# Retention attention and two mixtures of experts on one core: stores of x issued by POOL, copies of the x sums placed behind a block's layer 1 output, fewer staged pieces in expert 0, gate units at other places

## The chip, the cores and the metric

One core of a Trainium2 chip. Its engines are PE (matrix products), DVE, ACT and POOL (elementwise work) and SP, whose queue only issues transfers. Each engine takes its instructions strictly in order. The metric is the device time of one execution in microseconds (us).

## The reference

float32 throughout. The heads of the retention layer are laid side by side as 2304 rows of 512 and go through a dense mixture of 4 experts and then a routed one of 8, in which each row takes the expert of its largest logit.

```python
# retention, 4 batches, 8 heads, 576 positions, 64 wide
ret = scale * q @ k.T * Dmat          # Dmat[i, j] = gamma_h ** (i - j) for i >= j, else 0
x = (ret @ v)  ->  rows (2304, 512)
# mixture 1: 4 experts, all rows through each (512 -> 1024 -> 512)
for e in range(4):
    out += p[:, e:e+1] * (np.maximum(x @ w1[e], 0) @ w2[e])
# mixture 2: 8 experts, each row through one
logits = x @ w_gate; e_idx = argmax(logits); gate_w = softmax(logits)[e_idx]
eom = sigmoid(x @ w_output_gate)
out[mask] = gate_w * eom[:, e] * (np.maximum(x[mask] @ w1[e], 0) @ w2[e])
```

## The kernel before

**Numbers.** A float32 value is kept as a high and a low float16 part (`hi`, `lo`): ACT copies the high part, and POOL or DVE subtracts it from the value to get the low one. A product is three float16 products on PE.

**Blocks and units.** The 2304 rows are cut into 9 blocks of 256. Mixture 1 runs expert by expert, block by block. A block's layers are lists of units, a unit being some 12 to 24 matmuls. Blocks 0 to 4 of expert 0 use plain layers (`l1_first`, L518, and the second layer, L668); all later ones use layers with fewer products of sums and differences of quarters (`l1_mixed`, L546, and `l2_mixed`, L631), for which weights and x need such sums too. `keep` (L504, L505) takes a unit of layer 1 from PSUM: ACT writes the high part of ht (after the ReLU), DVE the low one.

**Attention inside expert 0.** The retention is computed in 36 steps of 64 positions, four steps to a block of x. Behind each unit of expert 0's first five blocks, `at_hook` runs one step s. It issues the loads of step s+4 on SP (qkr, vkr; five buffers), then `x_mix` of a block whose last step was s-1 (four subtractions on POOL, L347, that make the sums of x in place, `xf`), the step itself, `x_store` of the block's high and low parts (two steps behind its last), `x_keep` (three behind: the sums' high part by ACT, `xm`, L355, the low part by POOL, L356), and the second `x_store` (four behind). In a step PE takes the state of the past (L273), the scores of the next step (L250), their product with v (L286), and the next state (L301, from `ks`, which POOL scales, L229). DVE takes the step's result from PSUM as `xf` (L335), and ACT and POOL split it (L337, L339). The bank `uo` of a step is free for L273 of the next one once DVE has read it. Blocks of x later needed again are stored to DRAM as `xcd` (L359) and loaded by `x_load` (L383, or L385 and L386).

**Order.** A tile scheduler fixes the order on each engine before the run. A block `with tc.issue_after(i)` adds an edge: what is issued inside stands behind instruction i on the same engine. `pace` holds the last instruction of a kind for this. Other work is placed by tables of unit numbers: `w_plan` (weights of the next expert, with sums by POOL, `mix`, L449), `s_plan` (the weights of mixture 2, staged in pieces: load `sr`, two ACT instructions L200 and L201, one of DVE L202, store), and `gate_at` (units of mixture 2's gate and routing: `g1_rows`, `g1_turn`, `g2`, `g3a`, `g3b`). In the expert layers, POOL's L565, DVE's L569 and L606 and DVE's L639 (`acc`, the sum over experts) take units from PSUM.

Of the kernel before, what the change touches and what calls it, by code (L numbers as in the profile page):

```python
# [13 lines left out]
ACTF = mybir.ActivationFunctionType  # L14
ALU = mybir.AluOpType
# [11 lines left out]
NB = N // BT  # L27
# [16 lines left out]
BM = 5  # L44
# [86 lines left out]
def kernel(  # L131
# [19 lines left out]
    pe, act, dve, pool, sp = nc.tensor, nc.scalar, nc.vector, nc.gpsimd, nc.sync  # L151
# [58 lines left out]
    open_ctx = ExitStack()  # L210
    at_ps = [open_ctx.enter_context(tc.tile_pool(name="ps_1", bufs=2, space=PSUM))]
    ka = at_1.tile([128, ca.shape[1]], F32, name="ka", bufs=1)
    raws, pm, st, uos = {}, {}, {}, {}
    xcs, xfs, xos = {}, {}, {}

    def at_load(s):
        b, c = divmod(s, NC)
        a = at_raw.tile([128, 2, 4, C], F32, name="qkr")
        t = at_raw.tile([128, 2, 4, D], F32, name="vkr")
        sp.dma_start(out=a, in_=qk[b, c])  # L220
        sp.dma_start(out=t, in_=vk[b, c])
        raws[s] = a, t

    def at_split(s):
# [124 lines left out]
    def x_keep(b):  # L349
        m = xfs.pop(b)  # L350
        if xos[b][1] is None:
            xos[b][1] = at_1.tile([128, 2, 4, 2, HB], F16, name="xm", bufs=1)
        for i in range(2):
            hi, lo = [xos[b][1][:, a, 2 * i:2 * i + 2] for a in range(2)]
            act.activation(out=hi, in_=m[:, i], func=ACTF.Copy)  # L355
            pool.tensor_tensor(out=lo, in0=m[:, i], in1=hi, op=ALU.subtract)  # L356

    def x_store(b, i):
        sp.dma_start(out=xcd[b * 128:(b + 1) * 128, :, 4 * i:4 * i + 4], in_=xos[b][i])  # L359

    def at_step(s):

# [16 lines left out]
    def x_load(b, q, base=False):  # L379
        t = x_p.tile([128, 2, 8, 2, HB], F16, tag="xc", name="xc")  # L380
        src = xcd[b * 128:(b + 1) * 128]
        if base:
            q.dma_start(out=t[:, :, 0:4], in_=src[:, :, 0:4])  # L383
        else:
            q.dma_start(out=t[:, :, 0:2], in_=src[:, :, 0:2])  # L385
            q.dma_start(out=t[:, :, 3:], in_=src[:, :, 3:])  # L386
        xcs[b] = t
# [109 lines left out]

    hts = {}
    ops = {}
    pace = {}  # L500

    def keep(src, dst):

# [224 lines left out]
    def g1_rows(t, pl):  # L728

        xr = pl.tile([128, 2, DM], F16, tag="xr", name="xr")  # L730
        split_z(acc[:, t, 0:DM], xr[:, 0], xr[:, 1], S_X1)
        x1h[t] = xr

    def g1_turn(t, pl):
        xs = pl.tile([128, 2, KD, 128], F16, tag="xs", name="xs", bufs=2)
        sp.dma_start(
            out=xs.rearrange("p a k t -> p (a k) t"), in_=x1h[t].rearrange("p a d -> p (a d)"), transpose=True
        )
        x1h[t] = xs
# [478 lines left out]
    def s_plan(e, b, u):  # L1218
        if e == 0 and b <= BM:
            return  # L1220
        if b >= 2:
            if u in ((1, 3, 5, 7, 9, 12), (0, 3, 5, 7, 9), (0, 3, 5, 7, 9), (3, 5, 7, 9))[e] or (0 < e < 3 and b in (4, 6, 8) and u == 12):
                s_hook()
        elif b == 1 and u in (4, 6, 9):
            s_hook()
# [20 lines left out]
    def gate_plan(b):  # L1246
        ts = [b * TB + i for i in range(TB)]
        if b < NB - 3:
            for i, t in enumerate(ts):
                gate_at.setdefault((b + 2, i), []).append(lambda t=t: g1_rows(t, gp[0]))  # L1250
                gate_at.setdefault((b + 2, i + 1), []).append(lambda t=t: g1_turn(t, gp[0]))
                gate_at.setdefault((b + 2, i + 9), []).append(lambda t=t: g2(t))
            gate_at[b + 3, 2] = [lambda: g3a(b, gp[0])]
            gate_at[b + 3, 5] = [lambda: g3b(b, gp[0])]
        else:
            gate.extend(lambda t=t: g1(t, gp[0]) for t in ts)
            gate.extend(lambda t=t: g2(t) for t in ts)
            gate.append(lambda: g3a(b, gp[0]))
            gate.append(lambda: g3b(b, gp[0]))
            if b == NB - 3:  # L1260
                gate.append(go_early)

    prev = None
    for e in range(E1):
        for b in range(NB + (e == E1 - 1)):
# [16 lines left out]
            for u, unit in enumerate(units):  # L1282
                unit()
                z_from(e == 0 and b < BM and (b == 0 or u >= 4))
                if e == 0:
                    if u == 1 and b >= 2 or (b, u) == (1, 5):
                        x_load((b + 1) % NB, sp, base=b + 1 < BM)
                elif (e, b) == (1, 0):
                    if u == 0:
                        x_load(1, sp)  # L1290
                elif u == 0 and not last and (e, b) != (E1 - 1, NB - 1):
                    with tc.issue_after(pace["pool"].ins):
                        x_load((b + 1) % NB, pool)
                if e == 0:
                    for _ in range(1 + (b == 0 and u % 2)):
                        at_hook()
                if not last:
                    w_plan(e, b, u)
                    s_plan(e, b, u)
                if e == E1 - 1:  # L1300
                    for g in gate_at.pop((b, u), ()):
                        g()
                    if gate:
                        gate.pop(0)()
# [121 lines left out]
```

## Time and profile before

| | |
|---|---|
| median of 3 runs | 1043.08 us (1040.55 to 1043.15) |
| the profiled execution: its own time | 1045.07 us |
| its span in the trace | 1043.2 us |
| mean granted clock of PE | 0.986 |
| PE busy | 975.4 us, 94% |
| DVE, ACT, POOL busy | 586.0, 525.1, 400.9 us |

The span is the time between the first and the last instruction of the trace; the own time holds what lies around it too. In a row of the trace, "out<-in" names what an instruction writes and reads, and brackets give the idle time of its engine just before it and what ended that.

### The profile page before, as it was taken

The page shows a single profiled execution, that of the slowest core. Times are in us where ns is not written, and L with a number is a line of the kernel's source. Part 1 is how long each engine was busy: PE and PEld are TensorE (multiplying, and loading weights), DVE is VectorE, ACT ScalarE, POOL GpSimd, SP SyncE. Part 2 cuts the span into 40 slices and gives each one's busy share as a digit, 9 for nine tenths or more (in the row PEclk, how much of TensorE's full clock was granted, in tenths as well). Part 3 has the DMA queues.
Part 4 walks back from the last instruction along what each step waited for, and adds up shares of the span by engine and source line. Part 5 has one row for each costly group of instructions (what it writes and reads, how often), then busy time and mean ns, then how long its engine had stood idle before and what let it go on. Part 6 is the DMA issues. An engine that isn't in the chain of part 4 may idle for free. (4 is left out here: it accounts for less than half of the span.)

```text
span 1043.2 us, 31930 instructions
## 1 busy us (share of the span) xinstructions
PE 975.4 (94%) x13507; PEld 834.3 (80%) x13507; DVE 586.0 (56%) x1297; ACT 525.1 (50%) x1001; POOL 400.9 (38%) x414
## 2 busy tenths in 40 slices
PE   5869599999999999999999999999999999999995
PEld 5655466788889999999999999989988677777773
DVE  5634335157766677675777777788878512112111
ACT  4224234268867777685777776655653222222221
POOL 3684674253535432462542453323423121121111
PEclk9998899999999999999999999999999999999998
DMA  8746666336756658646567753677657435372692
GB/s 310 268 154 204 212 210 222 107 98 206 245 178 167 212 191 281 231 134 200 175 207 262 225 170 97 178 233 199 173 164 259 164 117 203 127 302 79 256 392 83
DMA packets 98244, 205.82 MB, mean 197 GB/s; under 512 B 21486, under 2 KB 41710, under 8 KB 95792
## 3 DMA queue, kind: packets, MB, share of 16 engines
q1 hardware_dynamic: 87680, 164.96, 47.4%
q0 software_dynamic: 10416, 38.76, 12.1%
q8 instruction: 108, 1.77, 0.7%
q14 instruction: 40, 0.33, 0.1%
HBM read 194.21 MB, written 52.99 MB: 237 GB/s over the span
## 5 line engine op out<-in xcount | busy, mean ns | idle before, releaser
L631 PEld LDWEIGHTS <-op 128*128 128x128 f16 x2604 | 245.9, 98 | 34.3 <-issue 9.2
L565 POOL TENSOR_TENSOR op<-sm,op 128x512 f16<-128x512 f32 x124 | 142.5, 1158 | 301.5 <-ACT op L564 289.3
L546 PEld LDWEIGHTS <-wm_a 128*128 128x128 f16 x3264 | 192.4, 98 | 11.2 <-issue 7.6
L546 PE MATMUL ph<-xc,wm_a 128*128 128x128 f16 x2112 | 132.2, 219 | 6.4 <-DVE pq L606 6.4
L564 ACT ACTIVATE op<-sm 128x512 f16<-128x512 f32 x124 | 77.4, 633 | 90.0 <-DVE sm L569 90.0
L1051 DVE SCALAR_TENSOR_TENSOR h_s<-p_h,h_s 128x512 f16<-128x512 f32 x40 | 27.7, 692 | 159.2 <-ACT h_s L1050 152.0
L1058 PE MATMUL p_y<-wm_a,h_s 128*128 128x512 f16 x480 | 107.2, 379 | 0.5 <-DVE h_s L1051 0.5
L202 DVE TENSOR_TENSOR s<-pz,s 128x512 f16<-128x512 f32 x128 | 86.2, 686 | 36.3 <-ACT s L201 36.2
L449 POOL TENSOR_TENSOR wr<-wr 128x512 f32<-128x512 f32 x64 | 81.0, 1271 | 48.8 <-ACT pz L200 31.3
L631 PE MATMUL px<-wm_a,op 128*128 128x256 f16 x744 | 91.4, 272 | 7.7 <-DVE acc L639 7.7
L631 PE MATMUL pv<-wm_a,op 128*128 128x256 f16 x792 | 97.5, 273 | 0.0
L1058 PEld LDWEIGHTS <-h_s 128*128 128x128 f16 x480 | 46.6, 98 | 52.4 <-DVE h_s L1051 0.7
L200 ACT ACTIVATE pz<-sr 128x512 f32<-128x512 f32 x128 | 76.1, 605 | 8.0 <-DMA sr<-in_w2s_dram 2.7
L546 PEld LDWEIGHTS <-wm_b 128*128 128x128 f16 x1296 | 76.9, 98 | 3.0 <-issue 1.6
L201 ACT ACTIVATE s<-pz 128x512 f16<-128x512 f32 x128 | 74.3, 597 | 1.0
L1061 POOL DMA_INDIRECT out_dram<-y_s,sidxm x17 | 17.3, 1017 | 146.5 <-ACT y_s L1060 137.9
L639 DVE SCALAR_TENSOR_TENSOR acc<-px,p_sb,acc 128x256 f32<-128x256 f32 x124 | 59.1, 477 | 12.9 <-PE px L631 8.0
L1050 ACT ACTIVATE h_s<-p_h 128x512 f16<-128x512 f32 x40 | 23.9, 597 | 79.3 <-PE p_h L1041 75.2
L1041 PEld LDWEIGHTS <-wm_b 128*128 128x128 f16 x1056 | 60.0, 98 | 2.9 <-issue 0.8
L1041 PE MATMUL p_h<-x_s,wm_b 128*128 128x128 f16 x1056 | 61.6, 219 | 0.5 <-issue 0.5
L504 ACT ACTIVATE op<-py 128x512 f16<-128x512 f32 x31 | 18.5, 596 | 83.7 <-PE py L546 83.7
L200 ACT ACTIVATE pz<-wr 128x512 f32<-128x512 f32 x100 | 59.4, 604 | 2.0 <-DVE wm_a L202 1.2
(200 smaller groups left out, 1726.6 us busy)
## 6 DMA issues: line engine op xcount, KB each, us to landing
wm_a<-w2d SPq DMA_DIRECT2D x20, 2048.0 KB, 9.2
wr<-in_w_dram SPq DMA_DIRECT2D x40, 512.0 KB, 5.9
wm_b<-w1d SPq DMA_DIRECT2D x10, 2048.0 KB
wm_a<-w1d SPq DMA_DIRECT2D x10, 2048.0 KB
sr<-in_w1s_dram SPq DMA_DIRECT2D x64, 256.0 KB, 4.4
w1d<-s SPq DMA_DIRECT2D x64, 256.0 KB, 5.6
sr<-in_w2s_dram SPq DMA_DIRECT2D x64, 256.0 KB, 3.4
w2d<-s SPq DMA_DIRECT2D x64, 256.0 KB, 3.3
```

What stands on the lines that cost most here:

```text
L200: act.activation(out=z, in_=raw, func=ACTF.Copy, scale=scale)
L201: act.activation(out=hi, in_=z, func=ACTF.Copy)
L202: dve.tensor_tensor(out=lo, in0=z, in1=hi, op=ALU.subtract)
L449: pace["pool"] = pool.tensor_tensor(out=quarter(e, n, k, to), in0=quarter(e, n, k, x), in1=quarter(e, n, k, y), op=op)
L546: pe.matmul(bank[:, i], lhsT=w[:, k, u, 128 * i:128 * i + 128], rhs=x[:, v, d, k], start=(first and i == 0 and n == 0), stop=(n == 5), ski ...
L564: act.activation(out=hi, in_=s, func=ACTF.Copy)
L565: pool.tensor_tensor(out=lo, in0=s, in1=hi, op=ALU.subtract)
L631: pe.matmul(out, lhsT=o[a][:, v, k], rhs=w[c][:, k, u], start=(first and n == 0), stop=(n == 11), skip_group_check=True,)
L639: dve.scalar_tensor_tensor(out=a, in0=src, scalar=p_sb[:, b * TB + i, e:e + 1], in1=a, op0=ALU.mult, op1=ALU.add)
L1041: pe.matmul(ph[:, j], lhsT=w[k][:, x, f * 128:(f + 1) * 128], rhs=xs[:, y, k], start=(n == 0), stop=(n == 3 * KD - 1),)
L1051: dve.scalar_tensor_tensor(out=lo, in0=ph, scalar=0.0, in1=hi, op0=ALU.max, op1=ALU.subtract)
L1058: pe.matmul(po, lhsT=h[:, a, k], rhs=w[k][:, b], start=(n == 0), stop=(n == 3 * KF - 1))
```

## The change

Five things change. The stores of x go from SP's queue to POOL's. The two copies of the x sums are issued behind the last ReLU of layer 1 that was issued so far. `x_load` in expert 0 is issued behind the last vkr load. Blocks 6 to 8 of expert 0 stage four pieces instead of six, and experts 1 and 2 a sixth piece in every block from the third on rather than only in three of them. In expert 3 the gate's units stand at other unit numbers.

```diff
-    raws, pm, st, uos = {}, {}, {}, {}
+    raws, pm, st, uos, pace = {}, {}, {}, {}, {}
...
         sp.dma_start(out=a, in_=qk[b, c])
-        sp.dma_start(out=t, in_=vk[b, c])
+        pace["sp"] = sp.dma_start(out=t, in_=vk[b, c])
...
-        for i in range(2):
-            hi, lo = [xos[b][1][:, a, 2 * i:2 * i + 2] for a in range(2)]
-            act.activation(out=hi, in_=m[:, i], func=ACTF.Copy)
-            pool.tensor_tensor(out=lo, in0=m[:, i], in1=hi, op=ALU.subtract)
+        with tc.issue_after(pace["act"].ins):
+            for i in range(2):
+                hi, lo = [xos[b][1][:, a, 2 * i:2 * i + 2] for a in range(2)]
+                act.activation(out=hi, in_=m[:, i], func=ACTF.Copy)
+                pool.tensor_tensor(out=lo, in0=m[:, i], in1=hi, op=ALU.subtract)
 
     def x_store(b, i):
-        sp.dma_start(out=xcd[b * 128:(b + 1) * 128, :, 4 * i:4 * i + 4], in_=xos[b][i])
+        pace["pool"] = pool.dma_start(out=xcd[b * 128:(b + 1) * 128, :, 4 * i:4 * i + 4], in_=xos[b][i])
...
-            if u in ((1, 3, 5, 7, 9, 12), (0, 3, 5, 7, 9), (0, 3, 5, 7, 9), (3, 5, 7, 9))[e] or (0 < e < 3 and b in (4, 6, 8) and u == 12):
+            if u in ((1, 4, 7, 9), (0, 3, 5, 7, 9), (0, 3, 5, 7, 9), (3, 5, 7, 9))[e] or (0 < e < 3 and b >= 3 and u == 12):
                 s_hook()
...
             for i, t in enumerate(ts):
-                gate_at.setdefault((b + 2, i), []).append(lambda t=t: g1_rows(t, gp[0]))
-                gate_at.setdefault((b + 2, i + 1), []).append(lambda t=t: g1_turn(t, gp[0]))
-                gate_at.setdefault((b + 2, i + 9), []).append(lambda t=t: g2(t))
-            gate_at[b + 3, 2] = [lambda: g3a(b, gp[0])]
-            gate_at[b + 3, 5] = [lambda: g3b(b, gp[0])]
+                gate_at.setdefault((b + 2, 2 * i + 2), []).append(lambda t=t: g1_rows(t, gp[0]))
+                gate_at.setdefault((b + 2, 2 * i + 3), []).append(lambda t=t: g1_turn(t, gp[0]))
+                gate_at.setdefault((b + 2, i + 12), []).append(lambda t=t: g2(t))
+            gate_at[b + 3, 1] = [lambda: g3a(b, gp[0])]
+            gate_at[b + 3, 4] = [lambda: g3b(b, gp[0])]
...
-                        x_load((b + 1) % NB, sp, base=b + 1 < BM)
+                        with tc.issue_after(pace["sp"].ins):
+                            x_load((b + 1) % NB, sp, base=b + 1 < BM)
```

How this moves instructions is shown at three places. The rows are those of the orders of before and of the change; line numbers of the change are one or two higher.

On ACT, in the first block with plain layer 1 units (from about 64 us of the profile before), before:

```order
L504 ACTIVATE ht<-ph 128x512
L355 ACTIVATE xm<-xf 128x512 x2
L337 ACTIVATE xo<-xf 128x4x64
L504 ACTIVATE ht<-ph 128x512
L337 ACTIVATE xo<-xf 128x4x64
L504 ACTIVATE ht<-ph 128x512
```

and now:

```order
L505 ACTIVATE ht<-ph 128x512
L337 ACTIVATE xo<-xf 128x4x64
L505 ACTIVATE ht<-ph 128x512
L337 ACTIVATE xo<-xf 128x4x64
L505 ACTIVATE ht<-ph 128x512
L356 ACTIVATE xm<-xf 128x512 x2
```

The two copies xm stood behind the block's first ht and stand behind its third.

On POOL, in the second layer of block 0 (about 36 to 53 us of the profile before), where wr are the weight sums, xc from L356 the low parts of the x sums, xc from L339 the low parts of a step's result, and ks the scaled keys, before:

```order
L339 TENSOR_TENSOR xc<-xf,xc 128x4x64 x2
L229 TENSOR_TENSOR ks<-vkr,ka 128x256
L449 TENSOR_TENSOR wr<-wr 128x512 x4
L339 TENSOR_TENSOR xc<-xf,xc 128x4x64
L229 TENSOR_TENSOR ks<-vkr,ka 128x256
```

and now:

```order
L339 TENSOR_TENSOR xc<-xf,xc 128x4x64 x2
L450 TENSOR_TENSOR wr<-wr 128x512
L357 TENSOR_TENSOR xc<-xf,xc 128x512 x2
L229 TENSOR_TENSOR ks<-vkr,ka 128x256
L360 DMA xcd<-xc 256x1x1024
L450 TENSOR_TENSOR wr<-wr 128x512 x7
L339 TENSOR_TENSOR xc<-xf,xc 128x4x64
L229 TENSOR_TENSOR ks<-vkr,ka 128x256
```

One weight sum and two low parts now stand ahead of the first ks, and a store and seven weight sums instead of four ahead of the second.

On DVE, in expert 3 (the cycle of about 697 to 702 us of the profile before), where L202 writes staged pieces (xr, s) and the rest are the gate's small instructions, before:

```order
L810 TENSOR_TENSOR g<-lg,oh 128x16
L812 TENSOR_REDUCE sg<-g 128x2
L202 TENSOR_TENSOR xr<-pz,xr 128x512
L639 SCALAR_TENSOR_TENSOR acc<-pv,p_sb,acc 128x256
L202 TENSOR_TENSOR s_12370<-pz,s_12370 128x512
L815 TENSOR_SCALAR se<-se 128x2
L817 RECIPROCAL iv<-se 128x4
L818 SCALAR_TENSOR_TENSOR acc<-iv 128x2
L202 TENSOR_TENSOR s_12416<-pz,s_12416 128x512
L639 SCALAR_TENSOR_TENSOR acc<-px_12260,p_sb,acc 128x256
L591 TENSOR_TENSOR pq<-ph,s_12342 128x512
L639 SCALAR_TENSOR_TENSOR acc<-px_12260,p_sb,acc 128x256
```

and now:

```order
L815 TENSOR_SCALAR se<-se 128x2
L818 RECIPROCAL iv<-se 128x4
L819 SCALAR_TENSOR_TENSOR acc<-iv 128x2
L640 SCALAR_TENSOR_TENSOR acc<-px_12260,p_sb,acc 128x256
L592 TENSOR_TENSOR pq<-ph,s_12338 128x512
L784 TENSOR_TENSOR cum<-pr,cum 128x8 x2
L788 TENSOR_TENSOR rk<-pr,cum 128x16
L202 TENSOR_TENSOR xr<-pz,xr 128x512
L791 TENSOR_TENSOR rk<-rk,oh 128x16
L640 SCALAR_TENSOR_TENSOR acc<-px_12260,p_sb,acc 128x256
L793 TENSOR_REDUCE rs<-rk 128x2
L202 TENSOR_TENSOR s_12448<-pz,s_12448 128x512
```

One xr and one s piece that stood ahead of the first acc<-px stand behind it.

## Rows read from the trace of the kernel before

**Rows 1.** The page, part 1 (busy us, share of the span, instructions) and part 2 (clock).

```profile
PE 975.4 (94%) x13507; PEld 834.3 (80%) x13507; DVE 586.0 (56%) x1297; ACT 525.1 (50%) x1001; POOL 400.9 (38%) x414
...
PEclk9998899999999999999999999999999999999998
```

**Rows 2.** Timeline of PE, 78 to 130 us (start us, us, instruction [idle before <-releaser]).

```profile
78.73 0.70 PE L273 MATMUL uo<-qkr,sn 64*64 64x64 f32 x16 [6.84 <-DVE xf L335]
...
81.05 1.46 PE L518 MATMUL ph<-xc,wm_c 128*128 128x256 f16 x6
...
85.76 0.46 PE L273 MATMUL uo<-qkr,sn 64*64 64x64 f32 x16
...
87.22 2.76 PE L668 MATMUL po<-wm_c,ht 128*128 128x512 f16 x12
...
121.51 0.69 PE L273 MATMUL uo<-qkr,sn 64*64 64x64 f32 x14 [10.37 <-DVE xf L335]
...
123.84 1.46 PE L518 MATMUL ph<-xc,wm_c 128*128 128x256 f16 x6
...
126.25 0.82 PE L518 MATMUL ph<-xc,wm_c 128*128 128x256 f16 x6
126.90 0.82 PE L518 MATMUL ph<-xc,wm_a 128*128 128x256 f16 x6
```

**Rows 3.** Timeline of all engines, 70.5 to 79 us (columns as in rows 2).

```profile
72.65 2.33 POOL L347 TENSOR_TENSOR xf<-xf 128x256 f32<-128x256 f32 x3
...
74.21 0.63 ACT L355 ACTIVATE xm<-xf 128x512 f16<-128x512 f32 x1 [9.65 <-POOL xf L347]
...
76.46 0.69 DVE L505 SCALAR_TENSOR_TENSOR ht<-ph,ht 128x512 f16<-128x512 f32 x1 [9.76 <-ACT ht L504]
```

**Rows 4.** Timeline of POOL, 30 to 125 us.

```profile
44.40 0.61 POOL L229 TENSOR_TENSOR ks<-vkr,ka 128x256 f32<-128x256 f32 x1 [3.66 <-DMA vkr<-in_vk_dram]
45.67 5.32 POOL L449 TENSOR_TENSOR wr<-wr 128x512 f32<-128x512 f32 x4 [0.65 <-DMA wr<-in_w_dram]
...
60.97 2.29 POOL L356 TENSOR_TENSOR xc<-xf,xc 128x512 f16<-128x512 f32 x2
```

**Rows 5.** Timeline of PE, 42 to 66 us.

```profile
52.59 0.47 PE L301 MATMUL uo<-vkr,ks 64*64 64x64 f32 x16
...
56.80 0.42 PE L301 MATMUL uo<-vkr,ks 64*64 64x64 f32 x16
...
60.40 0.46 PE L301 MATMUL uo<-vkr,ks 64*64 64x64 f32 x16 [0.54 <-POOL ks L229]
...
64.52 0.46 PE L301 MATMUL uo<-vkr,ks 64*64 64x64 f32 x16 [0.69 <-POOL ks L229]
```

**Rows 6.** Queue SP (SPq), waits at 40 to 200 us.

```profile
SPq L359 <- POOL xo L339: 38.9, 7, 11.8
```

**Rows 7.** Groups on POOL, 0 to 320 us: a load that POOL issues.

```profile
L386 POOL DMA_DIRECT2D xc<-xcd x2 | 1.5, 739 | 0.0
```

**Rows 8.** Waits of POOL, 0 to 320 us.

```profile
POOL wr L449 <- DMA wr<-in_w_dram: 16.1, 6, 8.5
```

**Rows 9.** Waits of PE, 0 to 320 us (us in total, times, longest).

```profile
PE ph L546 <- DVE pq L606: 5.7, 4, 2.0
PE ph L518 <- DVE ht L505: 3.1, 2, 2.1
```

**Rows 10.** Busy time (us) in two stretches: PE, PEld, DVE, ACT, POOL, clock, DMA share, GB/s.

```profile
256.00:276.00 20.00, 17.95 (x244) 16.85 (x242) 15.30 (x27) 17.11 (x34) 7.36 (x7) 1.00 0.91 308
...
470.00:640.00 170.00, 168.77 (x2292) 159.56 (x2290) 120.11 (x206) 120.12 (x228) 73.67 (x70) 1.00 0.62 196
```

**Rows 11.** Waits of PE, 640 to 820 us.

```profile
PE px L631 <- DVE acc L639: 7.6, 8, 1.2
```

**Rows 12.** Timeline of DVE, 688 to 702 us.

```profile
694.57 0.68 DVE L202 TENSOR_TENSOR xr<-pz,xr 128x512 f16<-128x512 f32 x1
...
699.29 0.48 DVE L639 SCALAR_TENSOR_TENSOR acc<-px,p_sb,acc 128x256 f32<-128x256 f32 x1
```

More of the change, by code (lines that the diff above doesn't have):

```diff
@@ L499 @@
     ops = {}
-    pace = {}
     def keep(src, dst):
```

## The prediction

> **What bounds the kernel now.** I read the page first: PE is busy 975.4 of 1043.2 us [rows 1], so nearly all that any change can win lies in its 68 us of idle time and in the slices where its clock is below 1 (the fourth, fifth and the first ones [rows 1]). The timeline of PE says where the idle time lies. Two stalls stand out, 6.84 us before 78.73 and 10.37 us before 121.51, both of L273, which waits for DVE's xf [rows 2]. The timeline of the other engines gives the chain behind the first one. DVE is no slow engine there: it had stood 9.76 us in front of its half of ht, which waits for ACT's half; and ACT had stood 9.65 us in front of the first xm copy, which waits for POOL's x_mix, whose last three pieces run from 72.65 to 75.0 [rows 3]. ACT runs in order, so the copy, which nobody needs soon, held ht, ht held DVE, DVE held xf, and xf held PE. The second stall has the same shape.
>
> Two smaller families of stalls follow. From block 6 of expert 0 into the first block of expert 1, PE waits 5.7 us in 4 places for DVE's pq [rows 9]; there ACT is busy 17.11 of 20 us [rows 10], since each staged piece puts two ACT instructions and one of DVE between the layers' work. In expert 3 PE waits 7.6 us in 8 places, 1.2 at most, for DVE's acc of a px bank [rows 11].
>
> **Part 1, the copies of the x sums.** In the new order on ACT the two xm copies stand behind three ht of the block instead of one. x_mix has until the third ht then, some two units and two attention steps later, about 8 us, so no ht waits for it. Both stalls go: 6.84 + 10.37 = 17.2 us. The clock goes with them. After the first stall the 24 matmuls of a unit took from 81.05 to 85.76, 4.71 us; at full clock six of them advance by 126.90 − 126.25 = 0.65, so 2.6 for 24: 2.1 lost. The attention step before it took 81.05 − 78.73 = 2.32 against 87.22 − 85.76 = 1.46: 0.9 lost. After the second stall a step took 123.84 − 121.51 = 2.33 (0.9 lost) and twelve matmuls 126.25 − 123.84 = 2.41 against 1.3 (1.1 lost) [rows 2]. Together 5.0 us. Bounds: 5.0 if PE stays busy, 0 if other stalls of some microseconds keep the clock low. I take all of it here, and charge the new stalls below. PE also waits 3.1 us in 2 places for DVE's ht directly, 2.1 the longer [rows 9]; of these I take 2.1 (0 to 3.1).
>
> **Part 2, the stores on POOL.** A store issued by POOL is not in the trace. The nearest row is a load that POOL issues, 0.74 us of POOL's time [rows 7]; 18 stores are 13 us, of a POOL that is busy 38% [rows 1], but not where they fall. From 45.67 on POOL works through weight mixes, 5.32 us in one stretch [rows 4], and PE's L301, which needs POOL's ks, waits 0.54 and 0.69 us at 60.40 and 64.52 [rows 5]. The new order there puts one wr mix and the two xc residues ahead of a ks, and one store and seven wr mixes ahead of the next. Prices: wr 5.32 / 4 rounded down for overlap to 1.27, residue 2.29 / 2 = 1.15, ks 0.61, mix 0.75 [rows 3, 4]; an x residue of one step I take at 0.68, as short as a ks and a little more. The first ks starts at 45.67 + 1.27 + 2.3 = 49.2 instead of 44.40; PE needs it at 52.59, so it hides. The next starts at 49.2 + 0.6 + 0.7 + 7 × 1.27 + 0.7 = 60.1, ready at 60.8, where PE wanted it at 56.80 [rows 5]: **4.0 us of new stall**. The third, behind three mixes, a residue and a store (3.7), is ready at 65.0, where PE, 4.0 late, wants it at 60.40 − 0.54 + 4.0 = 63.9: 1.1. The fourth, behind a mix, three residues and a store (4.5), at 70.1, where PE, 3.4 after the third, wants it at 68.4: 1.7. Sum 6.8, less the 1.2 that PE waits there now: 5.6 us (3.6 if the first weight load lands 2 us earlier, since one store less stands ahead of it on SP). A stall of 4 us, shorter than the two above, may cost some clock: between 0 and 3.0 (what followed the first one, [rows 2]), I take 1.5.
>
> In return the loads on SP no longer queue behind the stores. The stores stood 38.9 us in front of SP's queue in 7 places for POOL's xo alone, 11.8 at most [rows 6], with qkr and vkr loads behind them. The Trainium skill, "DMA: Bandwidth & Descriptors", section "Issuing engines are not separate DMA queues", holds that issuing from several engines saves only the sequencer's time to initiate, which is usually small; by that, part 2 would have no gain and the sum would be the same, since I give it none of its own. The trace disagrees with it as a full account here, since what the queue loses is waits (38.9 us), not issue time. I take the earlier vkr as what lets part 1's gain stand: with the stall gone, PE comes some 7 us earlier to a ks that would else wait for its load.
>
> **Part 3, x_load behind the vkr loads.** It goes three or four loads later in SP's order, still ten units or more ahead of the block that reads it, each 2.6 us and more: hidden, 0. Without this cover each of three blocks would begin with a wait for a load, up to the 8.5 us of the longest in the trace [rows 8].
>
> **Part 4, staged pieces.** Blocks 6 to 8 have 4 pieces instead of 6, which removes two of the units in which ACT and DVE are overfull. Of 5.7 us I take 3.5 (2 to 5). Experts 1 and 2 take three pieces more each; there PE idles 1.2 of 170 us with ACT busy 120.12 and DVE 120.11 [rows 10], so there is room: cost 1 (0 to 2.5).
>
> **Part 5, the gate units.** In the cycle shown DVE works without a gap until the px acc at 699.29, for which PE waits. The new order puts one xr and one s piece of L202, 0.68 us alone and 0.6 from start to start each, behind that add [rows 12], and one short reduction ahead of it: 1.0 us less. That is nearly all of a 1.2 us wait. Of 7.6 us [rows 11] I take 5 (2 to 7).
>
> **The sum.** 17.2 + 5.0 + 2.1 − 5.6 − 1.5 = 17.2 for parts 1 and 2; 3.5 − 1 for part 4; 5 for part 5: 24.7 us. From the profiled execution's own 1045.07 that is 1020.4. It ran 2.0 us above the median of 1043.08, so on the scale of the median **1018** (1018.4).
>
> **The rivals.**
> *POOL becomes the bound.* The ks stalls are not 6.8 but a chain: each one makes DVE's xf late, so x_mix and the stores behind it on POOL start later still, and the clock falls again. For it: POOL gets 9 us of wr in one run ahead of one ks. Against it: only some 3 us (four stores) are new work in all, the rest is order, and POOL idles later. Price: 6.8 twice and the clock's 3.0 twice instead of 5.6 + 1.5, 12.5 us worse: 1031.
>
> *The small parts don't pay.* ACT and DVE stay as full in blocks 6 to 8, with pieces merely later, and expert 3's add waits for another piece of the moved block. For it: DVE's total work in expert 3 is the same. Against it: a whole piece leaves each stretch ahead of the waiting unit. Price: 3.5 + 5 − 1 lost, 7.5: 1026.
>
> *The stores' move frees nothing,* because the loads wait for their buffers rather than behind a store. Then PE catches up with ks that wait for vkr, and part 1 turns half into waits for loads (3.7 us such a wait at 44.40 [rows 4], two or three in each block): 8 to 10 us worse, 1027.
>
> *Slower.* The run of wr mixes in front of a ks contains a wait: POOL waited 16.1 us in 6 places for a weight load, once 8.5 [rows 8]. In the new order four such runs (wr1 to 7, wr9 to 11, wr13 to 15 and the ones behind) stand ahead of a ks; if a load is late there, POOL's whole queue is late, all the attention steps behind it and PE too. It takes 24.7 + 3.1 = 27.8 us of such waits to be slower by 0.3%: three of 8.5 and the low clock behind each (about 2) give 31.5, so 1050. Against it: the weight loads no longer queue behind stores either.
>
> **How the numbers follow.** A difference of 0.3%, 3.1 us, is about what a measurement of this kernel tells from none. Forecast as worked out, 1018, within 1009 and 1025: 0.55. POOL bound, 1031: 0.15. Small parts don't pay, 1026: 0.08. Stores free nothing, 1027: 0.07. These are faster, 0.85. Slower, 1050 or so: 0.08. What is left, 0.07, is that gains and new stalls cancel. The range reaches from the forecast's lower end, with the bounds of the parts on the good side (ht 1.0, the new stall 2.0 and its clock 1.5, part 4 1.5 + 1, part 5 2: 9.0 better), 1009, to the rival on POOL with the bad bound of part 5 (3), 1034.
>
> **What the profile after would show.** Right: no row of L273 idle for 6 us or more between 70 and 125; xm copies on ACT with little wait; the clock full in the slices from 78 to 130 us; L301 waiting for ks some 4 us near 57 to 61; px waits in expert 3 below 0.5 each; fewer pq waits between 225 and 300. Wrong: PE's waits for ks or for xf add up to over 12 us before 200; POOL's rows of wr waiting for loads in front of a ks; px waits in expert 3 as long as before; new waits in experts 1 and 2 above 3 us.

## The result and the profile after

The changed kernel takes **1013.1 us** (median of 4 runs, 1009.4 to 1013.9) beside 1043.1 of the kernel before: a ratio of 0.9711 with a 95% interval from 0.9682 to 0.9739, 30 us less. The forecast was 1018, with a range from 1009 to 1034. The profiled execution took 1013.65 us with a span of 1011.8; 31.4 us less than that of before.

Where they went can be read from the start of the same matmul in the two timelines of PE, since the two programs run the same 13507 matmuls:

| start of | before | after | difference | in that stage |
|---|---|---|---|---|
| the first unit of L631, L632 after the change (end of the attention stretch) | 216.29 | 195.17 | -21.1 | -21.1 |
| the unit of L631 behind expert 0's last stall | 297.71 | 273.44 | -24.3 | -3.2 |
| a px unit in expert 2's sixth block | 574.98 | 550.34 | -24.6 | -0.4 |
| the first p_h (second mixture) | 809.50 | 776.69 | -32.8 | -8.2 |
| a p_y near the end (the 470th) | 1030.16 | 997.35 | -32.8 | 0.0 |
| the end of the span | 1043.2 | 1011.8 | -31.4 | +1.4 |

The last line is the landing of the last scattered output, which took a little longer in this execution; no instruction of PE stands behind it. The table compares one execution with one. In e4 below the attention stretch is as before, and its first unit of L631 starts at 211.93, 4.4 us ahead of before: so much of a stage's difference can lie between two executions.

The page of the changed kernel, parts 1 and 2 (busy us and share; granted clock in 40 slices), answers to [rows 1]:

```profile
PE 969.6 (96%) x13507; PEld 829.6 (82%) x13507; DVE 577.3 (57%) x1297; ACT 527.2 (52%) x1001; POOL 411.1 (41%) x432
...
PEclk9999999999999999999999999999999999999998
```

PE now idles 42 us instead of 68, and the two slices in which the clock read 8 read 9 like the others.

The waits of PE between 57 and 200 us (us in total, times, longest):

```profile
PE uo L301 <- issue: 2.0, 1, 2.0
PE uo L301 <- POOL ks L229: 1.7, 1, 1.7
```

These two lines are all that is left of the stretch in which the stalls of [rows 2] stood: no wait of L273 for xf. (What the first of them waits for, at 155.49, the trace does not show.) Why, the timeline of ACT shows (start us, us, instruction, and in brackets the idle time before it with what ended it):

```profile
63.41 0.59 ACT L505 ACTIVATE ht<-ph 128x512 f16<-128x512 f32 x1
...
70.20 0.60 ACT L505 ACTIVATE ht<-ph 128x512 f16<-128x512 f32 x1 [2.72 <-PE ph L519]
...
74.39 0.60 ACT L505 ACTIVATE ht<-ph 128x512 f16<-128x512 f32 x1 [0.99 <-PE ph L519]
74.88 1.14 ACT L356 ACTIVATE xm<-xf 128x512 f16<-128x512 f32 x2
```

The xm copies, which stood 9.65 us in front of ht [rows 3], stand behind the third ht and wait for nothing. That the second stall of before had the same shape as the first, the timelines of ACT and DVE of before show:

```profile
117.84 0.63 ACT L355 ACTIVATE xm<-xf 128x512 f16<-128x512 f32 x1 [11.90 <-POOL xf L347]
...
118.99 0.69 DVE L505 SCALAR_TENSOR_TENSOR ht<-ph,ht 128x512 f16<-128x512 f32 x1 [13.50 <-ACT ht L504]
```

In the changed kernel a later pair of copies still stands 8.32 us, at 123.61, but nothing that PE waits for stands behind it.

The new stall that the prediction charged is there, in its place but smaller. POOL's timeline at the same work as [rows 4], and the two rows of PE that answer to the last of [rows 5]:

```profile
41.13 1.26 POOL L450 TENSOR_TENSOR wr<-wr 128x512 f32<-128x512 f32 x1 [1.44 <-DMA wr<-in_w_dram]
42.35 2.27 POOL L357 TENSOR_TENSOR xc<-xf,xc 128x512 f16<-128x512 f32 x2
44.59 0.61 POOL L229 TENSOR_TENSOR ks<-vkr,ka 128x256 f32<-128x256 f32 x1
...
45.80 9.05 POOL L450 TENSOR_TENSOR wr<-wr 128x512 f32<-128x512 f32 x7
...
55.43 0.62 POOL L229 TENSOR_TENSOR ks<-vkr,ka 128x256 f32<-128x256 f32 x1
...
64.56 0.69 POOL L229 TENSOR_TENSOR ks<-vkr,ka 128x256 f32<-128x256 f32 x1
```

```profile
65.31 0.46 PE L301 MATMUL uo<-vkr,ks 64*64 64x64 f32 x16 [1.71 <-POOL ks L229]
65.70 4.46 PE L519 MATMUL ph<-xc,wm_a 128*128 128x256 f16 x24
```

The first weight mix starts at 41.13, not at 45.67: SP issued the load that it waited for at 34.60, and at 38.57 before. So the first ks starts at 44.59 (49.2 in the prediction), the ks behind the seven mixes (45.80, 9.05 us) is ready at 56.0 (60.8), and only the fourth ks is late, by 1.71 us where 4.0, 1.1 and 1.7 had been charged. The unit behind it took 4.46 us for 24 matmuls, some 1.7 more than the 2.79 at full clock (e11 below); the mean granted clock from 66 to 70 us was 0.60.

Groups of POOL in the attention stretch (busy us, mean ns), the price that no row of before showed:

```profile
L360 POOL DMA_DIRECT2D xcd<-xo x7 | 4.8, 685 | 0.0
```

0.685 us for a store; taken was 0.74 from [rows 7].

The smaller families, PE's waits at 200 to 320 us and at 640 to 820 us, beside [rows 9, 11]:

```profile
PE ph L547 <- DVE pq L607: 2.2, 3, 0.8
PE px L632 <- DVE acc L640: 0.9, 2, 0.4
```

```profile
PE px L632 <- DVE acc L640: 0.5, 2, 0.3
```

5.7 us became 2.2, and 7.6 us became 0.5.

### The profile page after: what moved, and what is told of

It reads as the page before. It is cut to its first block, busy times and chain, and to the rows that moved or that the text cites. A ratio compares the mean times of both kernels' runs of the same rounds, so it can differ in the third digit from the quotient of the medians.

```text
span 1011.8 us, 31937 instructions
## 1 busy us (share of the span) xinstructions
PE 969.6 (96%) x13507; PEld 829.6 (82%) x13507; DVE 577.3 (57%) x1297; ACT 527.2 (52%) x1001; POOL 411.1 (41%) x432
## 3 DMA queue, kind: packets, MB, share of 16 engines
q0 software_dynamic: 13008, 48.20, 14.9%
## 5 line engine op out<-in xcount | busy, mean ns | idle before, releaser
L632 PEld LDWEIGHTS <-op 128*128 128x128 f16 x2604 | 245.5, 98 | 27.0 <-issue 1.9
L565 ACT ACTIVATE op<-sm 128x512 f16<-128x512 f32 x124 | 77.4, 633 | 81.7 <-DVE sm L570 81.7
L202 DVE TENSOR_TENSOR s<-pz,s 128x512 f16<-128x512 f32 x128 | 85.4, 683 | 22.0 <-ACT s L201 22.0
L632 PE MATMUL pv<-wm_a,op 128*128 128x256 f16 x792 | 97.6, 273 | 0.0
L632 PE MATMUL px<-wm_a,op 128*128 128x256 f16 x744 | 91.4, 272 | 1.1 <-DVE acc L640 1.1
L1062 POOL DMA_INDIRECT out_dram<-y_s,sidxm x17 | 17.2, 1013 | 146.2 <-ACT y_s L1061 137.5
L201 ACT ACTIVATE s<-pz 128x512 f16<-128x512 f32 x128 | 73.7, 598 | 0.6
L1061 ACT ACTIVATE y_s<-p_y,x_g 128x512 f32<-128x512 f32 x20 | 13.7, 687 | 92.5 <-PE p_y L1059 78.9
```

Source lines behind the costliest of these rows:

```text
L201: act.activation(out=hi, in_=z, func=ACTF.Copy)
L202: dve.tensor_tensor(out=lo, in0=z, in1=hi, op=ALU.subtract)
L565: act.activation(out=hi, in_=s, func=ACTF.Copy)
L632: pe.matmul(out, lhsT=o[a][:, v, k], rhs=w[c][:, k, u], start=(first and n == 0), stop=(n == 11), skip_group_check=True,)
```

## The experiments

Medians, and ratios to the kernel before as run beside each group of kernels (1041.3 to 1044.0 us in the groups). Most executions lie within 3 us of their kernel's median, some further off (before: 1037.6 to 1046.8; one of e7's four at 1019.1); a trace shows where a wait stands, the median what it is worth.

| kernel | median us | ratio, 95% interval |
|---|---|---|
| changed | 1013.1 | 0.9711 (0.9682 to 0.9739) |
| e1: pin of the copies alone | 1035.4 | 0.9904 (0.9870 to 0.9938) |
| e2: stores on POOL alone | 1039.0 | 0.9953 (0.9931 to 0.9975) |
| e3: changed, stores back on SP | 1020.2 | 0.9779 (0.9743 to 0.9816) |
| e4: staged pieces and gate units alone | 1031.6 | 0.9882 (0.9849 to 0.9915) |
| e5: changed, each store as two | 1011.9 | 0.9707 (0.9664 to 0.9749) |
| e6: changed, x_load not pinned | 1017.0 | 0.9760 (0.9717 to 0.9803) |
| e7: changed, weight mixes behind the newest ks | 1012.1 | 0.9726 (0.9669 to 0.9783) |
| e8: changed, g3a and g3b where they were | 1014.8 | 0.9745 (0.9690 to 0.9800) |
| e9: e1 with the copies two steps later | 1033.4 | 0.9898 (0.9869 to 0.9928) |
| e10: changed, g1 and g2 where they were | 1015.8 | 0.9741 (0.9715 to 0.9768) |
| e11: as e7, only in the first steps | 1010.7 | 0.9684 (0.9661 to 0.9708) |
| e12: e3 with the stores issued later | 1016.9 | 0.9750 (0.9721 to 0.9779) |

**e1, the pin alone.** The theory was that the copies in front of ht made the two stalls; the rival, that late vkr behind the stores did.

```diff
# before, with
+        with tc.issue_after(pace["act"].ins):
             ... the copies of x_keep ...
```

> Before, with the copies of the x sums pinned behind the last ReLU of layer 1 and nothing else. Theory: the copies in front of ht made the two long stalls of L273, so the pin alone takes 17.2 us of stall and about 5 of clock, less 3 to 8 of waits for vkr loads that still queue behind the stores on SP: 1021 to 1030 us, and no L273 stall over 3 us between 60 and 125 us. Rival (the stores on SP were the cause, through late vkr, late ks and late x_mix): the copies wait for x_mix in any case and the gain is under 7 us: 1036 us or more.

Neither: 8.5 us. The first stall went as the theory has it (a matmul at 86.83 before starts at 74.42), and most of it came back at 96.52. The second one went too (the matmul of 121.51 starts at 110.25), and a wait of 3.55 us came at 130.54. One chain shows the stall at 96.52, from the timelines of SP, POOL, ACT, DVE and PE:

```profile
82.69 0.53 SPq L360 DMA_DIRECT2D xcd<-xm  x1
...
83.97 0.78 SPq L221 DMA_DIRECT2D vkr<-in_vk_dram  x1
```

```profile
79.83 0.61 POOL L229 TENSOR_TENSOR ks<-vkr,ka 128x256 f32<-128x256 f32 x1 [6.68 <-DMA vkr<-in_vk_dram]
...
89.29 0.61 POOL L229 TENSOR_TENSOR ks<-vkr,ka 128x256 f32<-128x256 f32 x1 [4.74 <-DMA vkr<-in_vk_dram]
...
90.61 2.32 POOL L347 TENSOR_TENSOR xf<-xf 128x256 f32<-128x256 f32 x3
```

```profile
92.96 1.15 ACT L356 ACTIVATE xm<-xf 128x512 f16<-128x512 f32 x2 [13.34 <-POOL xf L347]
...
94.84 0.57 ACT L201 ACTIVATE wm_a<-pz 128x512 f16<-128x512 f32 x1
...
95.45 0.69 DVE L202 TENSOR_TENSOR wm_a<-pz,wm_a 128x512 f16<-128x512 f32 x1 [12.32 <-ACT wm_a L201]
...
96.06 0.41 DVE L255 TENSOR_TENSOR pf<-sc,ka 128x256 f32<-128x256 f32 x1
...
96.52 0.70 PE L250 MATMUL sc<-qkr 64*64 64x64 f32 x16 [9.12 <-DVE pf L255]
```

Read it upward from PE. PE waits 9.12 us for pf; DVE, in order, had stood 12.32 us at a weight's low part (L202), which waits for ACT's L201; ACT had stood 13.34 us at the next pair of xm copies, which wait for x_mix; x_mix stands on POOL behind a ks that waited 4.74 us for its vkr (an earlier one had waited 6.68); and the vkr of the 4.74 us was issued at 83.97, behind a store at 82.69 for which SP waited until POOL had made the low parts of xm. So the stores and the copies hold the same thing in two ways: the copy holds whatever stands behind it on ACT (ht in the kernel before, a weight split here), for as long as x_mix is late, and x_mix is late because POOL waits for loads that SP holds behind a store for which POOL's own work must come first.

**e2, the stores alone.**

```diff
# before, with
-        sp.dma_start(out=xcd[...], in_=xos[b][i])
+        pool.dma_start(out=xcd[...], in_=xos[b][i])
```

> Before, with the stores on POOL's queue and nothing else. Theory: the xm copies still stand behind the first ht, x_mix comes a few us earlier at best, and POOL has 0.7 us more to do for each store: both L273 stalls stay, shortened by 0 to 5 us each: 1034 to 1045 us. Rival (the stores were the cause): the stalls go with the late vkr loads, 1028 us or less.

As the theory has it: 5.0 us. x_mix comes earlier, but the copies still hold ht. Both L273 stalls of [rows 2] stay, 3.42 and 8.69 us instead of 6.84 and 10.37, in the timeline of PE:

```profile
75.49 0.46 PE L273 MATMUL uo<-qkr,sn 64*64 64x64 f32 x16 [3.42 <-DVE xf L335]
...
118.55 0.70 PE L273 MATMUL uo<-qkr,sn 64*64 64x64 f32 x16 [8.69 <-DVE xf L335]
```

The loads are what the stores' move frees. POOL's waits for vkr at 30 to 200 us, first in e2, then in e1:

```profile
POOL ks L229 <- DMA vkr<-in_vk_dram: 3.3, 3, 2.0
```

```profile
POOL ks L229 <- DMA vkr<-in_vk_dram: 29.2, 6, 6.7
```

These waits are 2.7 us in the changed kernel and 3.3 in e2, with the stores on POOL, and 22.8 before, 17.9 in e3 and 29.2 in e1, with the stores on SP (12.8 in e12 and 9.5 in e9, where SP gets them later).

**e3, the stores back on SP.**

```diff
# changed, with
-        pace["pool"] = pool.dma_start(out=xcd[...], in_=xos[b][i])
+        sp.dma_start(out=xcd[...], in_=xos[b][i])
```

> The changed kernel with the stores back on SP's queue, all else kept. Theory: the loads of vkr queue behind stores again and ks is late in some steps, while POOL is spared 0.7 us a store and has fewer ks stalls near 57 to 67 us: 1016 to 1022 us. Rival (the stores carry the gain): 1030 us or more. Rival (the stores' move does nothing): within 1011 to 1015 us.

7.1 us longer, clear of the intervals, as the theory has it. In its trace one stall of 6.75 us stands at 93.50, with the chain of e1.

**e4, the late parts alone.**

```diff
# before, with the changed lines of s_plan and of gate_plan
```

> Before, with the staged pieces and the gate units of the change, and the attention stretch as before. If the late parts pay by themselves: 3.2 us in blocks 6 to 8 and 8.5 us in expert 3 as in the changed kernel's trace, 1030 to 1033 us. Rival (they only pay because the earlier stretch ends sooner and weights or loads are further ahead): under 6 us, 1037 us or more. Experts 1 and 2 unchanged in length within 0.5 us in either case.

They pay by themselves: 1031.6 us, a ratio of 0.9882. In its trace the stretch from the first unit of L631 to the one behind expert 0's last stall is 3.1 us shorter than before, and the one from expert 2's sixth block to the first p_h 8.1 us. So the attention parts together are worth 1031.6 - 1013.1 = 18.5 us, where e1 and e2 alone give 8.5 + 5.0 = 13.5. Taken by the ratios it is 17.8 for 14.9, each with several us of interval: that the two parts need each other is what the chain of e1 shows, and the medians alone would not.

**e5, twice as many stores on POOL.**

```diff
# changed, with
-        pace["pool"] = pool.dma_start(out=xcd[... :, ...], in_=xos[b][i])
+        for k in range(2):
+            pace["pool"] = pool.dma_start(out=xcd[... k:k + 1, ...], in_=xos[b][i][:, k:k + 1])
```

> The changed kernel with each store issued by POOL as two halves, so 36 issues instead of 18 for the same bytes. If POOL's own time for a store (0.68 us measured) is on the path only in the crowded stretch at 45 to 67 us, four more issues cost 2 to 4 us there and nothing later: 1014 to 1018 us. Rival (POOL is the bound of the whole attention stretch): all 18 count, 1023 us or more. Rival (stores on POOL are free): 1012 to 1014 us.

1011.9 us: no cost that shows. The group of e5 that answers to the one above:

```profile
L361 POOL DMA_DIRECT2D xcd<-xo x14 | 7.8, 558 | 0.0
```

0.56 us each for 36, so 20 us of POOL instead of 12, and PE's waits for ks rise only from 1.7 to 2.8 us. POOL isn't the bound of the stretch.

**e6, x_load without its edge.**

```diff
# changed, with
-                        with tc.issue_after(pace["sp"].ins):
-                            x_load((b + 1) % NB, sp, base=b + 1 < BM)
+                        x_load((b + 1) % NB, sp, base=b + 1 < BM)
```

> The changed kernel without the edge that holds x_load behind the last vkr load. As predicted (the place in SP's order is hidden): within 2 us of the changed kernel, 1011 to 1015 us. Rival (x_load waits for its stores in front of vkr loads, and so holds ks): 3 to 8 us longer, 1016 to 1021 us.

1017.0 us, 3.9 above the changed kernel by the median and in the rival's range, but the intervals overlap. The profiled execution was the fastest of the four (1013.93) and has one new stall, 2.60 us of L301 for ks at 103.75, with this on POOL ahead of it:

```profile
101.86 1.26 POOL L450 TENSOR_TENSOR wr<-wr 128x512 f32<-128x512 f32 x1 [7.93 <-DMA wr<-in_w_dram]
103.08 0.61 POOL L229 TENSOR_TENSOR ks<-vkr,ka 128x256 f32<-128x256 f32 x1
```

A weight mix stood 7.93 us for its load, in front of a ks. SP issued that load at 92.26, behind an x_load (L384, at 90.04) for which it had waited 6.9 us until a store of x had landed; in all it waited 16.3 us at x_load for stores, in 3 places, and not once in the changed kernel. POOL's waits for vkr rose from 2.7 to 8.9 us. Ahead of the stall this execution led the changed kernel's by 3.4 us, behind it it trailed by 2.6. This is the mechanism of the rival that ended slower, at one place and with a price of 6 us, and the waits at x_load are the ones that this experiment's own rival named. What the edge is worth over many executions is not shown.

**e7 and e11, the run of seven weight mixes broken.** e7 pins every weight mix behind the newest ks, e11 only those up to step 14.

```diff
# changed, with  pace["ks"] = pool.tensor_tensor(out=ks, ...)  and in mix
+        with tc.issue_after(pace["ks"].ins):        # e11: only while nxt[0] <= 15
             pace["pool"] = pool.tensor_tensor(out=quarter(e, n, k, to), ...)
```

> The changed kernel with each weight mix of POOL pinned behind the newest ks, which breaks the run of seven mixes. Theory (that run makes ks late near 57 to 67 us): the waits there (2.0 and 1.7 us) and the low clock behind them (1.7 us) go, 1008 to 1011 us. Rival (later weight mixes make weights late, ACT's splits of them hold ht): 1015 us or more. Rival (the stall moves to the next ks): within 1012 to 1014 us.

Within 1 us of the changed kernel by the median. The waits for ks near 65 us went, and PE is some 3 us ahead there; 1.8 of it is given back at 114.20, and the rest at 154 to 160, where a unit took 4.45 us that takes 2.76 in the changed kernel. The first give-back, in the timelines of ACT, DVE and PE:

```profile
111.00 0.60 ACT L200 ACTIVATE pz<-wr 128x512 f32<-128x512 f32 x1 [2.13 <-POOL wr L451]
...
112.27 0.69 DVE L202 TENSOR_TENSOR wm_a<-pz,wm_a 128x512 f16<-128x512 f32 x1 [2.34 <-ACT wm_a L201]
...
114.20 0.46 PE L273 MATMUL uo<-qkr,sn 64*64 64x64 f32 x16 [1.78 <-DVE xf L335]
```

A weight mix that now stands behind a ks is late for ACT's split (2.13 us), DVE waits 2.34 us for that in front of the step's sn and xf, and L273 waits 1.78. It is the chain of e1 again, from another late thing.

> The changed kernel with the weight mixes pinned behind the newest ks only up to step 14, where seven mixes stood in one run; later mixes as in the changed kernel. With the pin everywhere 2.9 us were won near 65 us and 2.3 given back later, 1.7 of them near 114 us where a weight split waited for a late mix. If the give-back came from the later pins alone, 2 to 3 us remain: 1009 to 1012 us. Rival (it is given back anyway, in the stretch behind): within 1 us of the changed kernel, 1012 to 1014 us.

1010.7 us in 5 runs (1009.0 to 1011.7). The fourth ks starts at 61.58 instead of 64.56, PE doesn't wait for it, and the unit behind the step runs at full clock:

```profile
65.75 0.42 PE L301 MATMUL uo<-vkr,ks 64*64 64x64 f32 x16
66.11 2.79 PE L522 MATMUL ph<-xc,wm_a 128*128 128x256 f16 x24
```

2.79 us for the 24 matmuls that took 4.46. Against the changed kernel's trace PE wins 3.6 us between 60 and 70 us; 1.0 of it is given back near 79 to 84, in two short waits (0.15 for a weight's low part, 0.76 for xf). The 3.6 can't be put down to the order alone: this execution came to the step 2.3 us later, and others with the seven mixes in one run waited 1.71 (e8), 1.20 (e10) and 0.36 us (e6) there, with 4.46, 2.79 and 2.79 us for the unit behind. By the medians e11 is 2.4 us better than the changed kernel; the intervals (0.9661 to 0.9708, 0.9682 to 0.9739) overlap, so it is a version that is at least as good, not one that is shown to be faster.

**e8 and e10, the gate's units apart.**

```diff
# e8: changed, with
-            gate_at[b + 3, 1] = [lambda: g3a(b, gp[0])]
-            gate_at[b + 3, 4] = [lambda: g3b(b, gp[0])]
+            gate_at[b + 3, 2] = [lambda: g3a(b, gp[0])]
+            gate_at[b + 3, 5] = [lambda: g3b(b, gp[0])]
# e10: the other way round, g1_rows, g1_turn and g2 at the units of before
```

> The changed kernel with g3a and g3b back at units 2 and 5 (g1 and g2 stay moved). In the changed kernel the px waits of expert 3 fell from 7.6 to 0.5 us. If it is g1's and g2's moving, which takes a staged xr out of the busy cycle, the waits stay below 2 us: 1012 to 1015 us. Rival (the key block of g3a, placed one unit earlier, opens the room): the 1.2 us waits come back in 5 or 6 blocks, 1018 to 1021 us.

> The changed kernel with only g3a and g3b moved, g1 and g2 back at their units of before. With only g1 and g2 moved the px waits of expert 3 were 3.0 us against 0.5 with both, and the stretch 2.9 us longer. If the two moves add up, g3 alone leaves about 5 us of px waits and the stretch 5.6 us longer than the changed kernel's: 1017 to 1020 us. Rival (g3's move alone is enough, g1 and g2 do what g3 does): under 1 us of px waits, 1012 to 1015 us.

1014.8 and 1015.8 us. Each move alone leaves 3.0 us of px waits in 7 places (0.5 with both, 7.6 with none), in e10 less than the 5 that were expected. The stretch from expert 2's sixth block to the first p_h is 2.9 us longer in e8 and 4.1 in e10 than in the changed kernel, 8.2 without either move. The medians are within the noise of the changed kernel's; the traces tell the two moves apart, below.

**e9, the copies two steps later, stores on SP.**

```diff
# e1, with
-        at_done(s - 4, x_store, 1)
-        at_done(s - 3, x_keep)
+        d = 5 if s <= NSTEP else 3
+        at_done(s - d, x_keep)
+        at_done(s - max(d, 4), x_store, 1)
```

> Before with the pin of the first experiment and, except for the last two blocks, the copies of the x sums issued two steps later (with the second store behind them); stores still on SP. In the first experiment a stall of 9.1 us near 96 us took the place of the one removed: the second pair of copies stood in front of a weight split on ACT, for which DVE waited. Theory (ACT's order carries that wait): with the copies behind the split and the next ht, the stall falls below 3 us, 1024 to 1031 us. Rival (late vkr loads behind the stores stall PE by themselves, through ks): a stall of similar size stays, 1033 us or more.

A miss: 1033.4 us. The stall at pf is gone, as the theory has it, but others of 4.09 and 6.73 us stand at 69.27 and 111.59, of L273 for xf, and the rival's time comes out without the rival's cause. DVE's waits between 60 and 130 us show why:

```profile
DVE xf L335 <- POOL xm L357: 7.9, 1, 7.9
...
DVE xf L335 <- POOL xc L357: 5.3, 1, 5.3
```

xf has two buffers. The low parts, two steps later, free one too late for DVE's next step. So the copies can come too early and too late: they belong behind the ht that PE needs, and ahead of the first xf of the block after next. The experiment moved them past that second bound, and does not tell how much of e1's loss the order on ACT alone makes.

**e12, stores on SP, issued later.**

```diff
# e3, with
-        at_done(s - 2, x_store, 0)
-        at_done(s - 4, x_store, 1)
+        at_done(s - 4, x_store, 0)
+        at_done(s - (5 if s <= NSTEP else 4), x_store, 1)
```

> The changed kernel with the stores on SP's queue, but issued one or two steps later (the first of a block behind its fourth step on, the second one step behind that), so that their data should be there when SP comes to them. If what SP costs is its waiting at a store in front of vkr loads, most of the 7 us between the changed kernel (1013) and the same with plain SP stores (1020) comes back: 1012 to 1016 us, with SP's waits at L360 below 20 us in all between 40 and 200 us. Rival (a store on SP costs by its place among the transfers, not by waits): 1018 to 1022 us with SP's waits at L360 equally small.

Inconclusive. 1016.9 us lies between, with an interval that meets both neighbours, and SP's waits at the stores did not fall: 41.9 us for xm and 33.4 for xo in its trace, which is of the slowest of the four executions (1020.65; the others 1013.9 to 1018.2). SP runs so far ahead that it waits at a store wherever it stands; POOL's waits for vkr fell only from 17.9 to 12.8 us. The sum of SP's waits was the wrong thing to ask for. What counts is whether a load that is soon needed stands behind the store.

## Why the prediction was right, and where its sizes were off

**What bounds the kernel**: right. Both stalls and the low clock behind them were the largest single thing to win, and the attention stretch gave 21.1 of 31.4 us (18.5 of 30.0 by the medians, e4).

**Part 1** (17.2 of stalls, 5.0 of clock, 22.2 together): the size is right. Around the two stalls of before, from 69 to 87 us and from 110 to 128, the changed kernel's PE wins 9.8 and 12.4 us, 22.2. The mechanism holds too, but the sum books all of it under the copies, and their pin alone gives 8.5 us (e1). The sentence that made part 1 depend on the stores' move, with no number of its own, was the important one: moving the stores back costs 7.1 us (e3). The rival that the stores' move frees nothing is excluded by that, and so is the rule of the Trainium skill, "DMA: Bandwidth & Descriptors", section "Issuing engines are not separate DMA queues", taken as the whole price of an issuing engine: it speaks of the sequencer's time to issue, and here 7.1 us hang on what waits in a queue behind a store. Of the 2.1 us for PE's waits at ht nothing came: the 2.09 us went and 2.42 us at 38.55 came, a wait of the second layer's first matmul for xf.

**Part 2** (5.6 us of new stall, 1.5 of clock) was mis-sized: the new waits for ks are 1.7 us, hardly more than the 1.2 of before, and the clock behind them costs 1.7. The step that was off is the start of the first weight mix, taken at 45.67 as before, with 2 us earlier as the bound; it started at 41.13, since SP issued its load 4 us earlier (34.60 for 38.57). Before, that load stood behind a qkr load that went out at 37.09, now that one went at 33.68; that it is the missing stores that did this is not shown. The earlier start took the 4.0 us at the second ks away and with it the 1.1 at the third; the 1.7 us at the fourth came as worked out. The price of a store (0.74 us taken, 0.685 measured) was right, and e5 shows that 8 us more of it cost nothing that shows. The rival that POOL becomes the bound is excluded by e5. e7 and e11 show that the wait at the fourth ks comes of the order, the seven mixes in one run: it is 1.71 us here, 0.36 to 1.71 in other executions, and the clock behind it is lost in some of them and not in others. What breaking the run is worth is 2.4 us by the medians, not clear of noise.

**Part 3** (0): that the later place is hidden is right, PE has no wait for a load of x in the changed kernel. That the edge could win something had no term; without it the median is 3.9 us longer, within the intervals, and SP waits at x_load in front of other loads (e6).

**Part 4** (3.5 won, 1 lost): 3.2 won, nothing lost in experts 1 and 2, and e4 shows the same without the other parts.

**Part 5** (5, bounds 2 to 7) was mis-sized: 8.2 us. The prediction took 1.0 us out of DVE's stretch ahead of the px add for a moved xr and s piece, which is what happened, and left the gate's own instructions at their length. They shrank too. Groups of DVE between 640 and 810 us (busy us, mean ns), in the kernel before and in the changed one:

```profile
L766 DVE TENSOR_TENSOR key<-key,kb 128x16 f32<-128x16 f32 x8 | 7.0, 871 | 0.0
...
L770 DVE TENSOR_TENSOR oh<-key,r 128x16 f16<-128x16 f32 x8 | 4.7, 587 | 0.0
L765 DVE TENSOR_TENSOR key<-lg,m 128x16 f32<-128x16 f32 x8 | 3.7, 467 | 0.3
```

```profile
L766 DVE TENSOR_TENSOR key<-lg,m 128x16 f32<-128x16 f32 x9 | 4.5, 502 | 0.3
...
L767 DVE TENSOR_TENSOR key<-key,kb 128x16 f32<-128x16 f32 x9 | 1.6, 174 | 0.0
L771 DVE TENSOR_TENSOR oh<-key,r 128x16 f16<-128x16 f32 x9 | 1.6, 173 | 0.2
```

The same three instructions of 16 columns, L766, L770 and L765 before and L767, L771 and L766 after, took 0.871, 0.587 and 0.467 us and take 0.174, 0.173 and 0.502 in the mean. These means mix two kinds of block: in the five whose px unit waited 1.2 us the three took 1.10, 0.84 and 0.56 us and take 0.17, 0.17 and 0.76, so 2.50 us became 1.11, another 1.4 us out of the stretch. That is a length set by POOL (last section). With over 2 us less in the stretch, a wait of 1.2 us is gone with room to spare. In e10, where g3's units alone are moved, these instructions keep their old lengths (0.794 and 0.541 for the two longest), in e8 they have the new ones (0.174 and 0.172): it is the moving of g1 and g2 that takes them from beside POOL's work, and both moves are needed to bring the px waits to 0.5 us.

**The sum**: 24.7 us forecast on the profiled execution's own time, 31.4 measured. By stages: the attention stretch 21.1 for 17.2 (22.2 for 22.2 around the two stalls, 2.5 lost up to 69 us where new stall, clock and ht had been put at 5.0, and 1.4 won later for which there was no term; by the medians of e4 and the changed kernel the stretch gave 18.5), blocks 6 to 8 3.2 for 3.5, experts 1 and 2 0.4 won for 1 lost, expert 3 8.2 for 5, and 1.4 lost at the end, for which there was no term. The forecast is 6.7 us short, most of it from part 2 (4.9 charged too much) and part 5 (3.2 given too little); ht and the end, which went the other way, hide some of that.

**The slower rival** did not come, but its mechanism is real: a weight mix waited 7.93 us in front of a ks in e6, at one place.

## What to carry to other kernels

On engines that run in order, look for the instruction that nobody needs soon and that stands in front of one that PE needs; a pin behind the needed one takes that wait away. It can be set too late as well (a buffer that comes free late, e9), and the next late thing then decides (e1). A store that waits for an engine's result should not stand in a queue in front of that engine's next inputs; issued by the engine that makes the data, it waited 0.3 us at a time here. Two half fixes of such a ring gave 8.5 and 5.0 us where both, with the edge of x_load, gave 18.5 (by medians of several runs each; the surplus of 5 is not clear of noise). When a planner's moves are priced by durations of before, ask which of them hold a wait for another engine.

## What the runs showed of the hardware

DVE's small instructions with two inputs from SBUF, if they begin while POOL's L565 runs, last until it ends; L565 reads sm and op from SBUF, not from PSUM. In the kernel before, in the cycle of [rows 12], from the timelines of DVE and POOL:

```profile
690.13 2.30 POOL L565 TENSOR_TENSOR op<-sm,op 128x512 f16<-128x512 f32 x2 [1.78 <-ACT op L564]
...
690.75 0.56 DVE L765 TENSOR_TENSOR key<-lg,m 128x16 f32<-128x16 f32 x1
...
691.35 1.10 DVE L766 TENSOR_TENSOR key<-key,kb 128x16 f32<-128x16 f32 x1
...
695.01 1.15 POOL L565 TENSOR_TENSOR op<-sm,op 128x512 f16<-128x512 f32 x1 [1.18 <-ACT op L564]
...
695.35 0.84 DVE L770 TENSOR_TENSOR oh<-key,r 128x16 f16<-128x16 f32 x1
```

The two POOL instructions that begin at 690.13 end near 691.3 and at 692.43; key ends at 691.31 and 692.45. POOL's next runs from 695.01 to 696.16; oh, begun at 695.35, ends at 696.19. So it goes in all five busy blocks, and the trace counts the wait as DVE's busy time. The same instructions take 0.17 us where POOL is idle (L767 and L771 above). DVE's L804, of the same size, begins at 691.24, just as one L565 ends and the next begins, and takes 0.16. The Trainium skill, "SBUF — State Buffer", section "SBUF: two separate sides", says that a DVE instruction with two SBUF inputs and a GpSimd one that reads SBUF exclude each other for a whole instruction, whichever starts first; this trace agrees, with 1.10 and 0.84 us for work of 0.17. The instructions of 512 columns of L202, which take one input from PSUM, keep their 0.68 to 0.69 us in both kernels, beside L565 or not.
